# Grouping the rows of two score rings by head, with the block-diagonal pads as plain copies

## The chip, the cores and the metric

The kernel runs on one core of one Trainium2 chip. The time is the device time of one execution in microseconds (us), as a median over several runs. A core has five engines that run their own instruction streams and wait for each other by semaphores: TensorE (PE, matmuls), VectorE (DVE), ScalarE (ACT), GpSimd (POOL) and SyncE (SP, which in this kernel issues nearly all DMAs). Sixteen DMA engines move data between device memory and the on-chip SBUF, which has 128 partitions; matmuls write to PSUM.

## The reference

The input x is one sequence of 2048 rows of 512 numbers. Two branches are mixed by a gate per row:

```python
g = sigmoid((x * gate_w).sum(-1, keepdims=True))
a = einsum("bsd,ed->bse", x, dft_hid_re);  b = einsum("bsd,ed->bse", x, dft_hid_im)
fourier = einsum("ts,bse->bte", dft_seq_re, a) - einsum("ts,bse->bte", dft_seq_im, b)
q, k, v = x @ wqkv                     # 32 heads of 16
scores = q k^T * 16 ** -0.5            # only 0 <= i - j < 256, else -1e9
attention = (softmax(scores) @ v) @ wo
out = g * fourier + (1 - g) * attention
```

So there is a Fourier branch of large dense products, and an attention of 32 small heads with a sliding window of 256 positions.

## The kernel before

**Number form.** Operands of the larger products are kept as a high and a low part in the fp32r type (`hi`, `lo`, `split`), and a product is three matmuls, hi·hi, hi·lo and lo·hi (`TERMS`). This holds for the projections to q, k and v, for the Fourier products and for the output product with wo.

**Attention tiles.** The 32 heads are four groups (`NG`) of four pairs (`NP`) of heads. The sequence is cut in blocks of 64 (`BQ`), so there are 32 blocks (`NB`) per group and 128 in all, counted by n. Two rings in SBUF, `ring[0]` for q and `ring[1]` for k, hold one group's values for 2048 positions; a partition is a row, and the free axis is (pair, position). Each of a pair's two heads has 16 rows of high and 16 of low parts, and rows of high parts are repeated so that one contraction over the partitions sums the three terms. Before the change the rows stand by part: 0-31 the high parts of both heads, 32-63 the low parts or the repeat, 64-95 the rest; rows 96-99 of `ring[0]` hold the row maxima that the transposed scores need.

A *pad* is the small stationary operand of a score matmul: for one block and pair, the columns 0-63 hold the 64 positions with head 0's rows only, and the columns 64-127 the same with head 1's rows only, so that one matmul gives both heads' scores. `make_pad` (L328 to L340) writes it from the ring, for all four pairs at once, by a multiplication with a 0/1 column `half` that blanks the other head's rows: two instructions per pad, of 96 rows each. `pads[0]` (from the q ring) serves `s_pair`, `pads[1]` (from the k ring) serves `t_pair`; there are two buffers of each (`NPAD`), so the pad of block n+2 cannot be written until the matmuls of block n are done. Three of the four instructions per block run on DVE (L339), the second of `pads[1]` on ACT (L337).

**Passes over a block.** `s_pair(n, p)` computes scores of 64 queries against up to 320 keys (L356), adds the mask and takes the minimum on DVE (L358), and exponentiates on ACT with a row sum (L361). Every eight blocks, the maxima and sums are split (`ml_split`), transposed on PE (`ml_turn`), and sent through device memory (`ml_rows`) into the rows of `ring[0]` (`m_ring`, L394). `LAG` = 19 blocks later `t_pair(k, p)` computes the transposed scores, 64 keys by up to 320 queries (L439), with the maxima subtracted in the same contraction, exponentiates on ACT (L440), and POOL zeroes the two triangular corners outside the window (`affine_select`, L445 and L449): two 64-row instructions per corner and two pairs, one for each head, since a head's keys stand in 64 partitions of their own. `pv` (L466) multiplies with v; its stationary operand `vpad` is again block-diagonal, spread by two POOL copies of 64 rows per four blocks (`v_spread`, L423) from `vr`, which two DMAs fill (`v_load`).

**The way of q and k.** A projection of 512 positions is accumulated in PSUM. `qk_evict` (L248) writes the high part with ACT (L84) and the low part with DVE (L86, L88) into one of three rotating slots of the tile `home`, and stores it to device memory (`qk_scr`) with one DMA of 128 partitions (512 KB). `ring_load` (L280) then brings q and k of 512 positions into the rings with four DMAs, of 64, 32, 32 and 64 partitions (512 or 256 KB). There are 16 ring loads, four per group. All these DMAs, and `ld` in general (L56), are issued by SP in program order, so one that waits holds up those behind it.

**Dense work between.** `dense()` is a generator that yields one matmul of the projections and Fourier products at a time. The main loop runs over n, and per pair emits the s matmul of block n, some dense matmuls (`fill`, 3 to 4 per pair), the t matmul of block n - 19, and more dense ones. The order on PE is thereby written out by hand. In the first part (L142 to L159) the orders of ACT, DVE and SP are, too; later they are set by a scheduler on estimated times, and `behind(...)` only fixes that an instruction is issued after the one marked last on an engine. The Fourier products over the sequence (`dc`) take their stationary operands from `raw` tiles with pieces of `cr` and `ci`, loaded and split one piece ahead (`Pieces`).

**Setup.** POOL builds the mask, the identity, `half` and `mrow`, zeroes rows 96-127 of the rings (`clear_rows`, L189), the corresponding rows of `pads`, and `vpad`; `clear_pads` (L201) sets rows of ones in `pads[1]`, to which the maxima rows of `ring[0]` answer.

Of the kernel before, what the change touches and what calls it, by code (L numbers as in the profile page):

```python
# [7 lines left out]
F32 = mybir.dt.float32  # L8
# [24 lines left out]
def fnet_window_mix(ctx: ExitStack, tc: tile.TileContext, xT, x, wqk, wv, wr, wi, cr, ci, wo, gw, out):  # L33
# [12 lines left out]
    qk_scr = [[[dram.tile([2, P, 512], F32, name=f"qk_scr{i}_{g}_{c}") for c in range(4)]  # L46
# [11 lines left out]
    def f(ap):  # L58
        return ap.bitcast(F32)
# [119 lines left out]
    half = const.tile([P, 2], F32, name="half")  # L179
    mrow = const.tile([P, 2], F32, name="mrow")  # L180
    for t, edges in ((half, ((0, 16, 32, 48, 64, 80), (16, 32, 48, 64, 80, 96))), (mrow, ((96, 98), (98, 100)))):
        nc.gpsimd.memset(t, 0.0)
        for h in range(2):
            for i, e in enumerate(edges[h]):
                a = t[:, h:h + 1]
                nc.gpsimd.affine_select(a, a, pattern=[[0, 1]], compare_op=OP.is_ge, fill=1.0 - i % 2,
                                        base=e - 1, channel_multiplier=-1)

    def clear_rows(i, ss):  # L189
        with behind("pool"):  # L190
            nc.gpsimd.memset(f(ring[i][96:128, :, ss * 512:(ss + 1) * 512]), 0.0)

    first_lo = f(XT[0, 0][96:128, 1]).rearrange("r (p c) -> r p c", p=NP)
    for t in pads[0]:
        mark("pool", nc.gpsimd.affine_select(t[96:128], first_lo, pattern=[[0, NP], [0, P]], compare_op=OP.is_gt,
                                             fill=0.0, base=0, channel_multiplier=0))
# [4 lines left out]
    def clear_pads():  # L201
        for t in vpad:
            nc.gpsimd.memset(t, 0.0)
        for t in pads[1]:
            nc.gpsimd.memset(f(t[96:128]), 1.0)
            for h in range(2):
                a = t[96:128, :, 64 * h:64 * h + 64]
                nc.vector.tensor_scalar(a, f(a), mrow[96:128, h:h + 1], None, op0=OP.mult)
# [39 lines left out]
    def qk_evict(g, ss, i, ps):  # L248
        hl = hl_tile()
        split_psum(hl[:, 0], hl[:, 1], ps, -SCALE if i == 0 else 1.0)  # L250
        ld(qk_scr[i][g][ss].rearrange("h x s -> x h s"), f(hl[:]))
# [76 lines left out]
    def make_pad(i, n):  # L328
        if not 0 <= n < NG * NB:
            return  # L330
        t = pads[i][n % NPAD]
        b = n % NB
        with behind(*(("act", "dve") if n < NPAD else ())):
            for h in range(2):
                src, dst = f(ring[i][:96, :, b * BQ:(b + 1) * BQ]), t[:96, :, 64 * h:64 * h + 64]
                if i and h:
                    nc.scalar.activation(dst, src, AF.Copy, scale=half[:96, h:h + 1])  # L337
                else:
                    nc.vector.tensor_scalar(dst, src, half[:96, h:h + 1], None, op0=OP.mult)  # L339
        PAD[i, n] = t  # L340
# [5 lines left out]
    def s_pair(n, p):  # L346
# [9 lines left out]
        nc.tensor.matmul(ps[:, :w], PAD[0, n][:, p], ring[1][:, p, k0:k0 + w], start=True, stop=True)  # L356
# [49 lines left out]
    def v_load(n):  # L406
        if n >= NG * NB:
            return
        g, kb = divmod(n, NB)
        raw = at.tile([P, 4, 64], F32, name="vr", bufs=1)  # L410
        for h in range(2):
            ld(raw[64 * h:64 * h + 64].rearrange("r (c j) x -> r c j x", j=2),
               v_scr[kb // 4][:, :, h, g, :].rearrange("c (j r) x -> r c j x", r=64))
        VR[n] = raw

    def v_spread(n):
# [4 lines left out]
        for h in range(2):  # L421
            r = slice(64 * h, 64 * h + 64)
            nc.gpsimd.tensor_copy(v2[r, :, :, 16 * h:16 * h + 16], raw[r].rearrange("r j (p d) -> r j p d", d=16))  # L423
        V2[n // 4] = v2

    def t_pair(n, p):
# [12 lines left out]
        nc.tensor.matmul(ps[:, :w], PAD[1, n][:, p], ring[0][:, p, q0:q0 + w], start=True, stop=True)  # L439
        nc.scalar.activation(pt[:, p, :w], ps[:, :w], AF.Exp, scale=-1.0)  # L440
        if p % 2:
            ph = slice(p - 1, p + 1)
            for h in (0, 64):
                a = pt[h:h + 64, ph, 0:64]
                nc.gpsimd.affine_select(a, a, pattern=[[0, 2], [1, 64]], compare_op=OP.is_ge, fill=0.0,  # L445
                                        base=0, channel_multiplier=-1)
                if w == WIN:
                    a = pt[h:h + 64, ph, 256:320]
                    nc.gpsimd.affine_select(a, a, pattern=[[0, 2], [-1, 64]], compare_op=OP.is_gt, fill=0.0,  # L449
                                            base=0, channel_multiplier=1)  # L450
# [479 lines left out]
```

## Time and profile before

| | |
|---|---|
| time, median of 3 runs | 853.65 us (852.76 to 855.3) |
| the profiled execution's own time | 853.36 us |
| its span in the profile | 851.3 us |
| PE busy | 844.4 us (99%) |
| DVE busy | 618.0 us (73%) |
| ACT busy | 592.0 us (70%) |
| POOL busy | 373.5 us (44%) |
| granted PE clock | 1.0 |
| moved by DMA | 161.03 MB, mean 189 GB/s |

A line of a group reads: line of the code, engine, operation, output tile <- input tiles, the shape (partitions x elements), the count, then busy time and mean ns of one, and the idle time of the engine just before them with what ended it. A line of a timeline gives the start, the duration and, in square brackets, the idle time before and who ended it. PE, DVE, ACT and POOL stand for the engines, PEld for loading a matmul's stationary operand, SPq for the DMA issues of SP. Matmuls overlap one another in the pipeline, so from one start to the next is less than the duration shown.

### The profile page before, as it was taken

The page shows a single profiled execution, that of the slowest core. Times are in us where ns is not written, and L with a number is a line of the kernel's source. Part 1 is how long each engine was busy: PE and PEld are TensorE (multiplying, and loading weights), DVE is VectorE, ACT ScalarE, POOL GpSimd, SP SyncE. Part 2 cuts the span into 40 slices and gives each one's busy share as a digit, 9 for nine tenths or more (in the row PEclk, how much of TensorE's full clock was granted, in tenths as well). Part 3 has the DMA queues.
Part 4 walks back from the last instruction along what each step waited for, and adds up shares of the span by engine and source line. Part 5 has one row for each costly group of instructions (what it writes and reads, how often), then busy time and mean ns, then how long its engine had stood idle before and what let it go on. Part 6 is the DMA issues. An engine that isn't in the chain of part 4 may idle for free.

```text
span 851.3 us, 17207 instructions
## 1 busy us (share of the span) xinstructions
PE 844.4 (99%) x5166; PEld 691.0 (81%) x5166; DVE 618.0 (73%) x2011; ACT 592.0 (70%) x1793; POOL 373.5 (44%) x1067
## 2 busy tenths in 40 slices
PE   8999999999999999999999999999999999999998
PEld 6888788788778888888878887888888887878887
DVE  5588978767878777769777787788888774447531
ACT  5488898888888987779778887778777765532200
POOL 9100244444543555456535546555355577740000
PEclk9999999999999999999999999999999999999999
DMA  7876577576675265444545556989774345359543
GB/s 247 284 235 203 179 247 237 205 238 215 208 240 173 68 210 122 153 129 139 154 114 151 164 144 205 294 275 287 254 216 145 111 148 162 120 170 317 159 147 98
DMA packets 94861, 161.03 MB, mean 189 GB/s; under 512 B 27312, under 2 KB 36272, under 8 KB 94768
## 3 DMA queue, kind: packets, MB, share of 16 engines
q1 hardware_dynamic: 94336, 159.28, 60.0%
q8 instruction: 40, 0.66, 0.3%
q10 hardware_dynamic: 432, 0.66, 0.2%
q14 instruction: 53, 0.43, 0.2%
HBM read 108.27 MB, written 51.64 MB: 188 GB/s over the span
## 4 chain that ended last, share of the span: by engine, by line
PE 94%; DVE 3%; DMA 2%; issue 1%; ACT 0%; SPq 0%; DVEq 0%; ACTq 0%
PE dc L518 41%; PE dab L294 10%; PE s L356 8%; PE o L466 8%; PE t L439 8%; PE dqk L271 7%; PE dv L294 5%; PE t L788 5%; DMA qk_scr<-home 1%; DVE sm L358 1%; DMA pt<-wqk 1%; PE s L259 0%; DVE pad L339 0%; DVE home L88 0%; DVE hi L574 0%
## 5 line engine op out<-in xcount | busy, mean ns | idle before, releaser
L361 ACT ACTIVATE sm<-sm,ml 128x320 f32<-128x320 f32 (+4 forms) x512 | 278.0, 544 | 101.7 <-DVE ml L358 96.5
L518 PE MATMUL dc<-big,hi 128*128 128x512 f32 x1020 | 344.4, 393 | 0.0
L358 DVE CUSTOM_DVE_ANT_0 sm<-s,mask 128x320 f32<-128x320 f32 (+4 forms) x512 | 235.1, 463 | 110.4 <-PE s L356 87.7
L445 POOL TENSOR_SCALAR_AFFINE_SELECT pt<-pt 64x128 f32<-64x128 f32 x392 | 137.1, 350 | 225.7 <-ACT pt L440 213.6
L518 PE MATMUL dc<-big,lo 128*128 128x512 f32 x510 | 200.6, 393 | 0.0
L518 PEld LDWEIGHTS dc<-big,hi 128*128 128x128 f32 x1020 | 179.7, 188 | 21.4
L440 ACT ACTIVATE pt<-t 128x320 f32<-128x320 f32 (+4 forms) x392 | 160.5, 411 | 43.9 <-PE t L439 41.2
L356 PE MATMUL s<-ring,pad 128*128 128x320 f32 (+4 forms) x512 | 157.6, 308 | 0.0
L439 PE MATMUL t<-ring,pad 128*128 128x320 f32 (+4 forms) x512 | 154.2, 301 | 0.0
L339 DVE TENSOR_SCALAR pad<-ring,half 96x256 fp32r<-96x256 f32 x384 | 119.9, 358 | 13.0 <-PE t L439 12.8
L356 PEld LDWEIGHTS s<-ring,pad 128*128 128x128 f32 x512 | 96.1, 188 | 30.2 <-issue 9.0
L449 POOL TENSOR_SCALAR_AFFINE_SELECT pt<-pt 64x128 f32<-64x128 f32 x344 | 119.7, 348 | 0.1
L439 PEld LDWEIGHTS t<-ring,pad 128*128 128x128 f32 x512 | 96.1, 188 | 21.9 <-DVE ml L358 0.7
L518 PEld LDWEIGHTS dc<-big,lo 128*128 128x128 f32 x510 | 95.8, 188 | 13.8 <-issue 1.6
L574 DVE TENSOR_TENSOR lo<-raw,hi 128x512 fp32r<-128x512 f32 x142 | 97.8, 698 | 0.1
L361 ACT ACTIVATION_READ_ACCUMULATOR sm<-sm,ml 128x1 f32 x512 | 97.6, 191 | 0.0
L294 PE MATMUL dab<-hi,big 128*128 128x512 f32 x256 | 89.4, 394 | 0.1
L271 PE MATMUL dqk<-big,hi 128*128 128x512 f32 x240 | 85.5, 394 | 0.8 <-DVE home L86 0.7
L423 POOL COPY vpad<-vr 64x256 f32<-64x256 f32 x64 | 27.7, 433 | 108.5 <-DMA vr<-v_scr 81.7
L574 DVE CAST hi<-raw 128x512 fp32r<-128x512 f32 x142 | 60.8, 437 | 18.9 <-PE dc L518 11.7
L445 POOL TENSOR_SCALAR_AFFINE_SELECT home<-home 64x128 f32<-64x128 f32 x120 | 44.3, 369 | 55.0 <-ACT home L440 47.9
L337 ACT ACTIVATE pad<-ring,half 96x256 fp32r<-96x256 f32 x128 | 63.9, 499 | 0.0
(96 smaller groups left out, 959.5 us busy)
## 6 DMA issues: line engine op xcount, KB each, us to landing
qk_scr<-home SPq DMA_DIRECT2D x32, 512.0 KB
ring<-qk_scr SPq DMA_DIRECT2D x32, 512.0 KB
raw<-cr SPq DMA_DIRECT2D x32, 512.0 KB
raw<-ci SPq DMA_DIRECT2D x32, 512.0 KB
r_scr<-ev SPq DMA_DIRECT2D x42, 256.0 KB
ev<-r_scr SPq DMA_DIRECT2D x42, 256.0 KB
ab_scr<-home SPq DMA_DIRECT2D x20, 512.0 KB
big<-ab_scr SPq DMA_DIRECT2D x20, 512.0 KB
```

The source lines that it names most:

```text
L271: nc.tensor.matmul(ps, w[a][:, c:c + 128], XT[dk, ss][:, b], start=n == 0, stop=n == 11)
L294: nc.tensor.matmul(ps, XT[dk, ss][:, a, c * 128:(c + 1) * 128], wh[b], start=n == 0, stop=n == 11)
L339: nc.vector.tensor_scalar(dst, src, half[:96, h:h + 1], None, op0=OP.mult)
L356: nc.tensor.matmul(ps[:, :w], PAD[0, n][:, p], ring[1][:, p, k0:k0 + w], start=True, stop=True)
L358: mark("dve", nc.vector.tensor_tensor_reduce(out=sm[:, :w], in0=ps[:, :w], in1=mask[:, WIN - w:], scale=1.0, scalar=3e38, op0=OP.add, op1= ...
L361: mark("act", nc.scalar.activation(sm[:, :w], sm[:, :w], AF.Exp, bias=nm[:, c], scale=-1.0, accum_out=l[:, c]))
L439: nc.tensor.matmul(ps[:, :w], PAD[1, n][:, p], ring[0][:, p, q0:q0 + w], start=True, stop=True)
L440: nc.scalar.activation(pt[:, p, :w], ps[:, :w], AF.Exp, scale=-1.0)
L445: nc.gpsimd.affine_select(a, a, pattern=[[0, 2], [1, 64]], compare_op=OP.is_ge, fill=0.0, base=0, channel_multiplier=-1)
L449: nc.gpsimd.affine_select(a, a, pattern=[[0, 2], [-1, 64]], compare_op=OP.is_gt, fill=0.0, base=0, channel_multiplier=1)
L518: nc.tensor.matmul(ps, w[a][:, i % 8 * 128:i % 8 * 128 + 128], ab[SC[i]][:, b], start=i == ends[0] and a + b == 0, stop=i == ends[1] and a ...
L574: return fn(*args)
```

## The change

The rows of rings and pads are grouped by head: head h has the 48 rows 64h to 64h+47, and the two maxima rows of a head follow at 64h+48. Rows between are zero in the pads. Then a block-diagonal pad is two plain copies of 48 rows, and nothing is to be blanked.

- `make_pad`: `pads[0]` is two DVE copies; `pads[1]` is two GpSimd copies, whose output has a stride of two, since in `pads[1]` the two heads now alternate: column 2r + h is key r of head h. ACT has no part of it any more.
- The transposed scores have keys of the two heads in alternating partitions, so one `affine_select` over 128 partitions per corner zeroes both heads' corners: half as many instructions as before.
- `v_load` is one DMA, and `v_spread` multiplies all 128 rows by the 0/1 column `side`, twice.
- `qk_scr` has an axis for the head; a store is two DMAs of 64 partitions (256 KB each) instead of one of 128. `ring_load` is eight DMAs, of 32, 16, 16 and 32 rows for each head, instead of four. `m_ring` is two DMAs of two rows instead of one of four.
- The s matmul contracts over 112 rows and the t matmul over 114, instead of 128.
- `half` and `mrow` are gone; `side` is a reduction of the identity on DVE and one more small instruction. `clear_rows` zeroes rows 32-63, before the ring loads write some of them; `clear_pads` sets ones and takes the other rows away with selects.

On PE the order of all matmuls is the same in both kernels. On SP two loads of `x` that stood ahead of a qk store near the end of the second group's projections stand behind it. POOL's pad copies stand among the selects of the block before, and the first of a pair waits for the t matmuls that last read its buffer.

```diff
 def clear_rows(i, ss):
-            nc.gpsimd.memset(f(ring[i][96:128, :, ss * 512:(ss + 1) * 512]), 0.0)
+            nc.gpsimd.memset(f(ring[i][32:64, :, ss * 512:(ss + 1) * 512]), 0.0)
...
 def qk_evict(g, ss, i, ps):
-        ld(qk_scr[i][g][ss].rearrange("h x s -> x h s"), f(hl[:]))
+        for h in range(2):
+            ld(qk_scr[i][g][ss][h].rearrange("a x s -> x a s"), f(hl[64 * h:64 * h + 64]))
...
 def ring_load(g, ss):
-        q, k = (qk_scr[i][g][ss].rearrange("h (x p) s -> (h x) p s", p=NP) for i in range(2))
-        ld(f(ring[0][0:64, :, sl]), q)
-        ld(f(ring[1][0:32, :, sl]), k[0:32])
-        ld(f(ring[0][64:96, :, sl]), q[0:32])
-        ld(f(ring[1][32:96, :, sl]), k)
+        for h in range(2):
+            r = 64 * h
+            q, k = (qk_scr[i][g][ss][h].rearrange("a (x p) s -> (a x) p s", p=NP) for i in range(2))
+            ld(f(ring[0][r:r + 32, :, sl]), q)
+            ld(f(ring[1][r:r + 16, :, sl]), k[0:16])
+            ld(f(ring[0][r + 32:r + 48, :, sl]), q[0:16])
+            ld(f(ring[1][r + 16:r + 48, :, sl]), k)
...
 def make_pad(i, n):
-                src, dst = f(ring[i][:96, :, b * BQ:(b + 1) * BQ]), t[:96, :, 64 * h:64 * h + 64]
-                if i and h:
-                    nc.scalar.activation(dst, src, AF.Copy, scale=half[:96, h:h + 1])
+                r = slice(64 * h, 64 * h + 48)
+                src = f(ring[i][r, :, b * BQ:(b + 1) * BQ])
+                if i:
+                    nc.gpsimd.tensor_copy(turned(t)[r, :, :, h], src)
                 else:
-                    nc.vector.tensor_scalar(dst, src, half[:96, h:h + 1], None, op0=OP.mult)
+                    nc.vector.tensor_copy(t[r, :, 64 * h:64 * h + 64], src)
...
 def s_pair(n, p):
-        nc.tensor.matmul(ps[:, :w], PAD[0, n][:, p], ring[1][:, p, k0:k0 + w], start=True, stop=True)
+        nc.tensor.matmul(ps[:, :w], PAD[0, n][:112, p], ring[1][:112, p, k0:k0 + w], start=True, stop=True)
...
 def m_ring(u):
-            ld(f(ring[0][96:100, :, U * 512:(U + 1) * 512]), m_scr[u])
+            for h in range(2):
+                ld(f(ring[0][64 * h + 48:64 * h + 50, :, U * 512:(U + 1) * 512]), m_scr[u][2 * h:2 * h + 2])
...
 def v_spread(n):
         for h in range(2):
-            r = slice(64 * h, 64 * h + 64)
-            nc.gpsimd.tensor_copy(v2[r, :, :, 16 * h:16 * h + 16], raw[r].rearrange("r j (p d) -> r j p d", d=16))
+            nc.gpsimd.tensor_scalar(v2[:, :, :, 16 * h:16 * h + 16], raw.rearrange("r j (p d) -> r j p d", d=16),
+                                    side[:, h:h + 1], None, op0=OP.mult)
...
 def t_pair(n, p):
-        nc.tensor.matmul(ps[:, :w], PAD[1, n][:, p], ring[0][:, p, q0:q0 + w], start=True, stop=True)
+        nc.tensor.matmul(ps[:, :w], PAD[1, n][:114, p], ring[0][:114, p, q0:q0 + w], start=True, stop=True)
-            for h in (0, 64):
-                a = pt[h:h + 64, ph, 0:64]
-                nc.gpsimd.affine_select(a, a, pattern=[[0, 2], [1, 64]], compare_op=OP.is_ge, fill=0.0,
-                                        base=0, channel_multiplier=-1)
+            a = pt[:, ph, 0:64]
+            nc.gpsimd.affine_select(a, a, pattern=[[0, 2], [2, 64]], compare_op=OP.is_ge, fill=0.0,
+                                    base=1, channel_multiplier=-1)
```

The new helper `turned(t)` views a pad's 128 columns as 64 pairs: `t[:].rearrange("x p (r h) -> x p r h", h=2)`.

More of the change, by code (lines that the diff above doesn't have):

```diff
@@ L44, in fnet_window_mix @@
     dram = ctx.enter_context(tc.tile_pool(name="dram", bufs=1, space=DRAM))
-    qk_scr = [[[dram.tile([2, P, 512], F32, name=f"qk_scr{i}_{g}_{c}") for c in range(4)]
+    qk_scr = [[[dram.tile([2, 2, 64, 512], F32, name=f"qk_scr{i}_{g}_{c}") for c in range(4)]
                for g in range(NG)] for i in range(2)]
@@ L410, in v_load @@
         raw = at.tile([P, 4, 64], F32, name="vr", bufs=1)
-        for h in range(2):
-            ld(raw[64 * h:64 * h + 64].rearrange("r (c j) x -> r c j x", j=2),
-               v_scr[kb // 4][:, :, h, g, :].rearrange("c (j r) x -> r c j x", r=64))
+        ld(raw.rearrange("r (c j) x -> r c j x", j=2),
+           v_scr[kb // 4].rearrange("c (j r) h g x -> g (r h) c j x", r=64)[g])
         VR[n] = raw
```

37 lines of the change are left out of this document (17 added, 20 removed).

## The prediction

> **What bounds the kernel.** I read the page first, then busy time by stage, then the waits around the stages where TensorE (PE) is not full.
>
> ```profile
> span 851.3 us, 17207 instructions
> PE 844.4 (99%) x5166; PEld 691.0 (81%) x5166; DVE 618.0 (73%) x2011; ACT 592.0 (70%) x1793; POOL 373.5 (44%) x1067
> PE 94%; DVE 3%; DMA 2%; issue 1%; ACT 0%; SPq 0%; DVEq 0%; ACTq 0%
> ```
>
> ```profile
> 20.00:60.00 40.00, 40.00 (x189) 33.11 (x188) 28.07 (x104) 23.82 (x74) 5.32 (x12) 1.00 0.85 271
> 60.00:100.00 40.00, 38.80 (x188) 32.65 (x187) 36.53 (x141) 33.45 (x102) 0.86 (x3) 1.00 0.57 181
> 100.00:140.00 40.00, 39.94 (x243) 32.20 (x242) 32.27 (x112) 34.75 (x108) 20.13 (x60) 1.00 0.75 244
> 140.00:700.00 560.00, 559.89 (x3650) 459.82 (x3652) 442.89 (x1520) 447.61 (x1397) 284.41 (x836) 1.00 0.59 183
> 700.00:760.00 60.00, 60.00 (x445) 47.76 (x435) 27.23 (x54) 31.10 (x76) 42.20 (x121) 1.00 0.43 138
> ```
>
> The columns are the window, its length, then busy time of PE, weight loads, VectorE (DVE), ScalarE (ACT) and GpSimd (POOL), the granted clock, and DMA share and GB/s. PE is the bound everywhere at clock 1.00. From 20 to 760 us it is idle 1.20 + 0.06 + 0.11 = 1.4 us. The matmuls of the changed kernel are as many and as wide, so whatever relieves another engine can win at most about 1.4 us. What makes a transfer or a copy late has no such cap.
>
> **Relief of DVE and ACT.** Before, a block (64 keys or queries of 8 heads) has three pad copies on DVE and one on ACT; after, it has two shorter ones on DVE (pad 0) and two on POOL (pad 1).
>
> ```profile
> L339 DVE TENSOR_SCALAR pad<-ring,half x384: 332/345/510, 33.8 to 754.1; 96x256 fp32r<-96x256 f32 x192
> ...
> L337 ACT ACTIVATE pad<-ring,half 96x256 fp32r<-96x256 f32 x128 | 63.9, 499 | 0.0
> ...
> L369 DVE CAST mlh<-ml x16: 181/191/320, 63.5 to 690.1; 128x64 fp32r<-128x64 f32 x16
> ...
> L80 DVE CAST big<-raw x8: 417/421/427, 23.6 to 52.2; 128x512 fp32r<-128x512 f32 x8
> ```
>
> ```profile
> 93.55 0.27 PE L376 MATMUL s<-ident,mlh 128*64 128x128 f32 x1 [0.54 <-DVE mlh L370]
> ...
> 99.31 0.50 PE L271 MATMUL dqk<-big,hi 128*128 128x512 f32 x1 [0.65 <-DVE home L86]
> ```
>
> A plain copy of 256 elements is interpolated between the CASTs: 191 + 192 x (421 - 191)/448 = 290 ns against 345. Until pad 1 begins, a block saves DVE 2 x 55 ns = 0.11 us; from then on 3 x 345 - 2 x 290 = 0.455 us. ACT loses its 63.9 us, which free no PE time as ACT is 0% of the chain above. The two PE waits on DVE shown fall at 93.55, where one or two blocks' 0.11 us can have gathered (I take 0.15 of the 0.54), and at 99.31, where pad 1 has begun (one and a half blocks' 0.455, so nearly all of the 0.65: 0.6). Term: **-0.75 us** (bounds 0 and -1.4).
>
> **GpSimd.** It gains two pad copies per block and loses half its selects, each twice as many partitions.
>
> ```profile
> L423 POOL COPY vpad<-vr x64: 390/399/1263, 90.2 to 740.5; 64x256 f32<-64x256 f32 x64
> ...
> L445 POOL TENSOR_SCALAR_AFFINE_SELECT pt<-pt x392: 286/293/1148, 102.8 to 763.8; 64x128 f32<-64x128 f32 x196
> ...
> L176 POOL TENSOR_SCALAR_AFFINE_SELECT ident<-ident x1: 294/294/294, 2.5 to 2.5; 128x128 fp32r<-128x128 f32 x1
> ```
>
> ```profile
> 8.65 14.08 POOL L191 MEMSET ring<- 32x2048 f32 x8
> ...
> 724.53 0.85 POOL L423 COPY vpad<-vr 64x256 f32<-64x256 f32 x2 [1.50 <-DMA vr<-v_scr]
> ```
>
> ```profile
> 7.06 1.15 DVE L81 TENSOR_TENSOR big<-pt,big 128x512 fp32r<-128x512 f32 x1 [1.20 <-ACT big L78]
> ```
>
> A select of 128 partitions costs what one of 64 does (294 against 293 ns); so a block's POOL work goes from 8 x 0.293 = 2.34 us to 4 x 0.294 + 2 x 0.399 = 1.97 us. No row has the strided output of pad 1; at the longest copy, 1.263 us each, a block would be 3.7 us, and the 128 blocks (selects from 102.8 to 763.8) are 5.2 us apart. In the end phase, 700 to 760 us, they are nearer: 121 POOL instructions are some 15 blocks, 4 us each with 42.20/15 = 2.8 us of POOL work, which becomes 2.8 x 1.97/2.34 = 2.4. A pad-1 copy waits for the last t of block k and is needed by the first t of block k + 2, so about a block lies between: hidden. Behind a waiting copy on POOL stand the next selects, for which pv waits some blocks later: hidden too. The thin place is the end, where v_spread waits for its load (the 1.50 above) and pad copies queue behind it; without cover that costs its 1.5 us there. The v_spread instructions stay 64, now of 128 partitions at the price of 64, as the selects show. The zeroing of the ring (14.08/8 = 1.76 us each) must now precede the ring loads; the two that matter end near 8.65 + 3.52 = 12.2 us, and the loads issue at 19.67 (below): hidden by 7 us, also with the pads' longer clearing ahead of it. Term: **0** (0 to +1.5). The new reduce and scalar on DVE fall into its startup idle of 1.20 us (last row): 0; without that cover they would be two small instructions, under 0.4 us by the 191 ns CAST.
>
> **Matmul rows.** s and t contract over 112 and 114 rows instead of 128.
>
> ```profile
> 97.90 0.31 PE L356 MATMUL s<-ring,pad 128*128 128x320 f32 x1
> 98.04 0.39 PE L271 MATMUL dqk<-big,hi 128*128 128x512 f32 x1
> 98.27 0.39 PE L271 MATMUL dqk<-big,lo 128*128 128x512 f32 x1
> ```
>
> All rows of the trace contract over 128, so they do not price this. Start to start, 320 columns take 0.14 us and 512 columns 0.23, the same time per column: the width sets it, and I take **0** (no row suggests a loss; the gain, if rows counted, is a rival). The Trainium skill, "TensorE: Matmul & The Clock Gate", section on LDWEIGHTS, says the row count does not matter for a weight load; no run here shows it yet.
>
> **Transfers.** The ring load (1.573 MB for 512 positions) was four DMAs over partitions 0-63, 0-31, 64-95 and 32-95; it becomes eight, of 32, 16, 16 and 32 rows, each wholly in 0-63 or wholly in 64-127. The qk store (0.524 MB) was one DMA over 128 partitions; it becomes two of 64.
>
> ```profile
> 19.67 3.16 SPq L56 DMA_DIRECT2D ring<-qk_scr  x4
> ...
> 25.38 0.39 SPq L56 DMA_DIRECT2D raw<-xT  x1
> ```
>
> ```profile
> 33.17 0.76 DVE L80 CAST big<-raw 128x512 fp32r<-128x512 f32 x2 [2.96 <-DMA raw<-xT]
> 33.85 0.60 DVE L339 TENSOR_SCALAR pad<-ring,half 96x256 fp32r<-96x256 f32 x2
> ```
>
> ```profile
> 34.51 0.30 PE L356 MATMUL s<-ring,pad 128*128 128x64 f32 x1
> ```
>
> ```profile
> 24.00:25.00 1.00, 1.00 (x6) 0.84 (x5) 0.96 (x3) 0.03 (x1) 1.00 (x4) 1.00 1.06 203
> ...
> 32.00:33.00 1.00, 1.00 (x7) 0.81 (x6) 0.00 (x0) 0.19 (x1) 0.00 (x0) 1.00 1.04 404
> ```
>
> ```profile
> 50.00:51.00 1.00, 1.00 (x6) 0.83 (x5) 1.00 (x4) 0.80 (x3) 0.00 (x0) 1.00 1.03 217
> 51.00:52.00 1.00, 1.00 (x7) 0.87 (x6) 1.00 (x5) 1.00 (x4) 0.00 (x0) 1.00 1.06 221
> 52.00:53.00 1.00, 1.00 (x7) 0.83 (x6) 1.00 (x5) 1.00 (x4) 0.00 (x0) 1.00 1.07 229
> ```
>
> With the DMA engines full (share 1.0 and above), the kernel moves 404 GB/s while xT lands on 128 partitions, and about 222 GB/s (217, 221, 229) while a ring load's one-sided pieces land. By these two rates a ring load before is (0.524 + 0.262 + 0.262)/0.222 + 0.524/0.404 = 6.0 us, the last piece straddling both sides; after it is 1.573/0.222 = 7.1 us: **+1.1**. A qk store goes from 0.524/0.404 = 1.3 to 2.36 us: **+1.06**. Bounds: if consecutive pieces of opposite sides overlap, a ring load is 1.573/0.404 = 3.9 us (-2.1) and a store +0. If 16 rows run at half of 32 rows' rate again, four of the eight pieces (0.524 MB) take another 2.36 us: +3.5. I take one after another at 222, the rate that both a 64-row and a 32-row piece show.
>
> *Start.* Two stores and one ring load stand in the queue before the xT load, whose landing lets DVE cast at 33.17, then copy the pad at 33.85, then PE do its first s at 34.51, back to back: no slack. Extra: 2 x 1.06 + 1.1 = **+3.2 us** (0 to +5.6; a gain is worth nothing, since PE runs full up to there). SP issues six DMAs more at about 3.16/4 = 0.79 us, 4.7 us, which moves the issue of xT (25.38) by at most that; it lands almost 8 us after its issue, behind what is queued, so the transfers and not SP set it. The v stores behind it on SP are read some 50 us later (first v copy at 90.2).
>
> *Group turn near 110 us.* PE resumes at 118.02 on a chain whose longest piece is a transfer:
>
> ```profile
> 103.59 2.77 SPq L56 DMA_DIRECT2D ring<-qk_scr  x4
> 106.46 1.02 SPq L56 DMA_DIRECT2D raw<-x  x2
> ```
>
> ```profile
> 107.58 8.98 DMA qk_scr<-home
> ...
> 116.64 0.61 ACT home L84
> ...
> 117.27 0.70 DVE home L88
> ...
> 118.02 0.49 PE dab L294
> ```
>
> The store issued at 107.58 has the store before it, a ring load and raw<-x ahead of it, and the next eviction needs its slot of home. Extra: 2 x 1.06 + 1.1 = 3.2; the two raw<-x loads (0.524 MB, 1.3 us at 404) are now queued behind, so **+1.9 us** (0 to +4.3).
>
> *Later ring loads.* Of the others, those in the dc phase stand before loads of cr and ci, which the pieces are split from with one piece of lead; the trace has one place where the cast waits:
>
> ```profile
> 592.22 0.43 DVE L574 CAST hi<-raw 128x512 fp32r<-128x512 f32 x1 [0.61 <-DMA raw<-ci]
> ```
>
> The load is late there and PE does not stall, so +1.1 is mostly covered: **+0.2** (0 to +2). The m_ring pieces (+16 DMAs) and the v loads (-32) hang on nothing near.
>
> **Sum** against the profiled execution's 853.36 us (span 851.3; the median of the runs is 853.65, 0.3 above): 853.36 - 0.75 + 0 + 0 + 3.2 + 1.9 + 0.2 = 857.9, rounded to 858.0.
>
> **Rivals.**
> *The 16-row pieces halve again.* Then a ring load costs +3.5, the start 2 x 1.06 + 3.5 = +5.6 and the turn 5.6 - 1.3 = +4.3: 853.36 - 0.75 + 5.6 + 4.3 + 0.2 = 862.7. For it: rows fell from 404 to 222 when partitions halved from 128 to 64. Against: 32-row pieces at 52 us run no slower than 64-row ones (229 against 217). Chance 0.22. The Trainium skill, "SBUF — State Buffer", "Door 1: The DMA port swizzle", makes the rate go by how many of 16 ports the partitions reach: rows 0-31 or 0-63 reach eight, rows 0-15 or 32-47 four; by it the sum would be this rival's. The trace agrees for eight against sixteen; none of its large transfers reach just four.
>
> *The transfers are hidden or the sides overlap.* For it: DMA share 0.57 to 0.85 leaves room, and 16 engines each with a queue of its own need not stay in step. Against: the full share at 24 to 34 us with no slack behind. Only the relief is left: 853.36 - 0.75 + 0.2 = 852.8. Chance 0.27.
>
> *Faster: rows count.* If a matmul's time falls with the rows it contracts, 1024 matmuls at 0.14 us of spacing (143 us together) save up to 12%, 17 us; it decides from 7.1 us on, 5% of them, since 4.5 is needed to undo the sum above and 2.6 more to be seen: 853.36 - 0.75 + 5.3 - 17 = 841 at the most. For it: no row excludes it. Against: the equal time per column above. Chance 0.06.
>
> *GpSimd late at the end or at every block.* With copies of 1.26 us a block of the end phase has 2.4 + 2 x 0.86 = 4.1 us of POOL work in 4 us, and t waits from there on: about 0.1 us a block and 1.5 us at each of three or four v_spreads, on hidden transfers 852.8 + 1.5 + 3 x 1.5 = 858.8. Chance 0.06.
>
> **How the numbers follow.** Main forecast 0.39. The 0.3% that a measurement tells from no change is 2.6 us. Slower: main 0.36 (its low end, with part of the transfers hidden, is within: 0.03), halving 0.22, GpSimd 0.05 = 0.63. Same: 0.03 + 0.25 + 0.01 = 0.29. Faster: rows 0.06 and 0.02 of the hidden case = 0.08. The main case's own range is 855.5 to 860.5. The range 852.0 to 863.5 leaves out the rows case, the lowest of the hidden one and the highest of the halving.
>
> **What would show it.** Right: in the 24 to 34 us windows the rate stays near 220 GB/s for over 7 us; the first s stands about 3 us later; the store at the group turn lands later than 8.98 us after issue and PE waits there; pad copies on DVE near 290 ns and no PE wait on POOL. Wrong: s and t spaced closer, the first s still at 34.5, waits of t on POOL, or rates above 300 GB/s while a ring load lands.

## The result: 28 us slower, and the profile after

The changed kernel takes 882.41 us (median of 4 runs, 880.75 to 894.15), against 854.19 us of the kernel before: a ratio of 1.0316, 95% interval 1.0285 to 1.0346. In a second set of runs it took 881.80 us against 853.10, a ratio of 1.0329 (1.0265 to 1.0393). The direction was forecast; the size, 858.0 us with a range up to 863.5, was not.

One of the first four executions, that of 894.15 us, was in a slower state and the ratio leaves it out; as the first profile is of that execution, the lines below are from the second profile, of an execution of 879.73 us. From the page of the changed kernel, the span, the engines and the chain:

```profile
span 878.0 us, 16821 instructions
...
PE 860.1 (98%) x5166; PEld 697.6 (79%) x5166; DVE 610.4 (70%) x1881; ACT 552.6 (63%) x1665; POOL 355.1 (40%) x831
...
PE 83%; DMA 8%; DVE 3%; issue 2%; SPq 2%; ACT 1%; POOL 1%; DVEq 0%; ACTq 0%
```

Busy time by stage (window, length, PE, weight loads, DVE, ACT, POOL, granted clock, DMA share, GB/s):

```profile
20.00:60.00 40.00, 36.40 (x170) 29.87 (x169) 24.21 (x89) 20.34 (x64) 5.85 (x9) 1.00 0.86 213
60.00:100.00 40.00, 38.59 (x184) 31.95 (x183) 33.87 (x132) 31.47 (x101) 1.86 (x2) 1.00 0.84 212
100.00:140.00 40.00, 36.79 (x185) 28.94 (x184) 29.39 (x95) 29.45 (x90) 12.30 (x32) 0.96 0.84 213
140.00:700.00 560.00, 555.98 (x3553) 452.72 (x3554) 431.41 (x1395) 411.16 (x1277) 260.57 (x634) 1.00 0.67 183
```

Two things are to be seen, against the first profile of the kernel before. The span grew by 26.7 us, but PE's idle time only by about 11 us (878.0 - 860.1 = 17.9 against 6.9): PE's *busy* time grew by 15.7 us, for the same 5166 instructions. And the DMA engines are busier for what they move: in the stage from 20 us the share is the same, 0.86 for 0.85, at 213 GB/s instead of 271; in the next it rose from 0.57 to 0.84 while the rate rose only from 181 to 212. The busy time is made up of longer steps at the s and t matmuls (experiment 5) and of a lower clock after standstills (the last point of the steps below).

The three longest places where PE stands still and the kernel before does not, then what ended them. At the start xT lands behind the ring load; at the group turn a store of q or k does; in the dc phase a piece of cr:

```profile
38.07 0.27 PE L358 MATMUL s<-ring,pad 112*128 112x64 f32 x1 [1.83 <-issue]
...
125.54 0.42 PE L441 MATMUL t<-ring,pad 114*128 114x320 f32 x1 [2.78 <-ACT pt L442]
...
566.65 0.51 PE L441 MATMUL t<-ring,pad 114*128 114x320 f32 x1 [2.80 <-DVE ml L360]
```

```profile
36.69 0.76 DVE L80 CAST big<-raw 128x512 fp32r<-128x512 f32 x2 [4.75 <-DMA raw<-xT]
...
565.13 0.43 DVE L575 CAST hi<-raw 128x512 fp32r<-128x512 f32 x1 [4.11 <-DMA raw<-cr]
```

```profile
109.51 7.00 DMA ring<-qk_scr
116.53 7.40 DMA qk_scr<-home
...
554.23 10.88 DMA raw<-cr
...
565.48 0.28 DVE pad L341
```

In the last chain DVE's cast waits for the piece of cr, and behind the cast, in DVE's order, stand a pad copy and the mask of s, without which the next matmul has no PSUM slot.

Where the time is lost becomes plain when each matmul of PE, whose order is the same in all these kernels, is compared with the same matmul in the second profile of the kernel before (span 852.9, experiment 11). The lag is how much later it starts, in us, worked out from the start times in the traces:

```
matmul no. (its time before)   changed   before, 112/114 rows   changed, 128 rows and transfers of before
  80  ( 23.2 us)                 -0.3           0.0                   0.1
 150  ( 40.3 us)                  1.9           0.2                  -1.8
 500  (114.2 us)                  3.5           0.5                  -1.8
 600  (131.4 us)                  8.4           0.8                  -1.7
3300  (543.4 us)                 14.8           6.9                  -1.8
3500  (571.9 us)                 19.5           7.1                  -1.8
4460  (720.2 us)                 23.5          10.4                  -1.8
```

The changed kernel loses in steps at the start, the group turn and the first ring load of the dc phase, and besides at a steady rate between 131 and 543 us, where no standstill is. The other two columns are the experiments that took these two losses apart (5 and 8). The -1.8 of the last column is mostly the kernel before: its second profile has a standstill of 1.60 us that ends at 27.27 us, and its first profile and the kernel of the last column have none there.

### The profile page after: what moved, and what is told of

It reads as the page before. It is cut to its first block, busy times and chain, and to the rows that moved or that the text cites. A ratio compares the mean times of both kernels' runs of the same rounds, so it can differ in the third digit from the quotient of the medians.

```text
span 892.4 us, 16821 instructions
## 1 busy us (share of the span) xinstructions
PE 864.6 (97%) x5166; PEld 699.5 (78%) x5166; DVE 610.4 (68%) x1881; ACT 552.9 (62%) x1665; POOL 357.1 (40%) x831
## 4 chain that ended last, share of the span: by engine, by line
PE 84%; DMA 10%; DVE 3%; issue 1%; POOL 1%; ACT 1%; SPq 0%; DVEq 0%; ACTq 0%; POOLq 0%
PE dc L519 35%; PE dab L295 9%; PE s L358 8%; PE dqk L270 8%; PE o L467 7%; PE t L441 7%; PE t L789 5%; PE dv L295 4%; DMA raw<-ci 2%; DMA ring<-qk_scr 2%; DMA vr<-v_scr 2%; DMA raw<-cr 1%; DMA raw<-xT 1%; DMA qk_scr<-home 1%; DVE sm L360 1%
## 5 line engine op out<-in xcount | busy, mean ns | idle before, releaser
L441 PE MATMUL t<-ring,pad 114*128 114x320 f32 (+4 forms) x512 | 156.7, 306 | 15.8 <-DVE ml L360 9.7
L339 POOL CAST pad<-ring 48x256 fp32r<-48x256 f32 x256 | 124.6, 487 | 107.3 <-PE t L441 87.8
L358 PE MATMUL s<-ring,pad 112*128 112x320 f32 (+4 forms) x512 | 159.5, 311 | 4.3 <-DVE pad L341 3.6
L446 POOL TENSOR_SCALAR_AFFINE_SELECT pt<-pt 128x128 f32<-128x128 f32 x196 | 65.1, 332 | 166.7 <-ACT pt L442 160.8
L441 PEld LDWEIGHTS t<-ring,pad 114*128 114x128 f32 x512 | 96.4, 188 | 39.8 <-DVE ml L360 10.6
L358 PEld LDWEIGHTS s<-ring,pad 112*128 112x128 f32 x512 | 96.6, 189 | 36.3 <-issue 14.2
L424 POOL TENSOR_SCALAR vpad<-vr,side 128x256 f32<-128x256 f32 x64 | 60.6, 957 | 125.6 <-DVE lo L575 63.1
L341 DVE CAST pad<-ring 48x256 fp32r<-48x256 f32 x256 | 98.8, 386 | 6.8 <-DMA ring<-qk_scr 2.9
L442 ACT ACTIVATE home<-t 128x320 f32<-128x320 f32 (+4 forms) x120 | 48.8, 408 | 18.8 <-PE t L441 18.0
L467 PE MATMUL o<-pt,vpad 128*32 128x320 f32 (+4 forms) x1072 | 58.7, 358 | 0.0
```

The lines of the kernel that those rows point to most:

```text
L339: nc.gpsimd.tensor_copy(turned(t)[r, :, :, h], src)
L341: nc.vector.tensor_copy(t[r, :, 64 * h:64 * h + 64], src)
L358: nc.tensor.matmul(ps[:, :w], PAD[0, n][:112, p], ring[1][:112, p, k0:k0 + w], start=True, stop=True)
L441: nc.tensor.matmul(ps[:, :w], PAD[1, n][:114, p], ring[0][:114, p, q0:q0 + w], start=True, stop=True)
L467: nc.tensor.matmul(OT[g, sb][32 * p:32 * p + 32, q - sb * 512:e - sb * 512], v2[:, p], pt[:, p, q - q0:e - q0], start=first, stop=kb == 8 ...
```

## The experiments

Theories: A, the shapes of the transfers make loads late; B, GpSimd's new work makes t late; and, formed later from the traces, C, matmuls over fewer than 128 rows take longer.

**1. The transfers of the change inside the kernel before.** The store as two DMAs of 64 partitions, the ring load as eight pieces, four of them of 16 rows:

```diff
...
-        ld(f(ring[0][0:64, :, sl]), q)
-        ld(f(ring[1][0:32, :, sl]), k[0:32])
-        ld(f(ring[0][64:96, :, sl]), q[0:32])
-        ld(f(ring[1][32:96, :, sl]), k)
+        ld(f(ring[0][0:32, :, sl]), q[0:32])
+        ld(f(ring[1][0:16, :, sl]), k[0:16])
+        ld(f(ring[0][32:48, :, sl]), q[32:48])
+        ld(f(ring[1][32:64, :, sl]), k[0:32])
+        ld(f(ring[0][64:96, :, sl]), q[0:32])
+        ld(f(ring[1][16:32, :, sl]), k[16:32])
+        ld(f(ring[0][48:64, :, sl]), q[48:64])
+        ld(f(ring[1][64:96, :, sl]), k[32:64])
```

> The kernel before, with only its transfers cut like those of the change: the qk store as two DMAs of 64 partitions, the ring load as eight DMAs of 32 and 16 rows, each on one side of partition 64. Layout, pads, selects and matmul rows are those of before. Theory A (the shapes of the transfers cost the time, the 16-row pieces most, through late loads at the start, at the group turn and in the dc phase): 870 to 884 us, with windows near 115 GB/s at a full DMA share while a ring load lands. Theory B (GpSimd's pad copies and its longer v spread make the t matmuls late, the transfers cost only what was forecast for them): 855 to 859 us.

Measured: 866.86 us, ratio 1.0151 (1.0103 to 1.0198), so some 13 us: about half of the loss, and B's 855 to 859 for this kernel is out. Theory A alone, which expected 870 or more, falls short as well.

**2. The same with six pieces of 32 rows** (0-31, 32-63 and 64-95 of each ring).

> The kernel before, with the qk store as two DMAs of 64 partitions and the ring load as six one-sided DMAs of 32 rows, so without 16-row pieces. Theory A, if it is the 16 rows that cost: 855 to 861 us, as the main forecast had it for one-sided pieces at 222 GB/s. If instead one-sided pieces and their number cost as such: 868 us and more. Theory B: 855 to 859 us here as well, and no difference between this and the kernel with 16-row pieces.

Measured: 856.41 us, 1.0031 (1.0008 to 1.0055): 2.6 us. One-sided pieces alone cost little; with 16-row pieces among them it is 10 us more. The rate tells why. One ring load in a quiet stretch, in the second profile of before, then with 32-row pieces, then in the changed kernel:

```profile
52.00:53.00 1.00, 1.00 (x6) 0.83 (x6) 1.00 (x6) 0.79 (x4) 0.00 (x0) 1.00 1.09 231
...
56.00:57.00 1.00, 1.00 (x7) 0.87 (x6) 1.00 (x5) 1.00 (x3) 0.00 (x0) 1.00 1.14 422
```

```profile
57.00:58.00 1.00, 1.00 (x7) 0.82 (x6) 1.00 (x4) 1.00 (x5) 0.00 (x0) 1.00 1.03 193
...
59.00:60.00 1.00, 1.00 (x7) 0.83 (x5) 0.64 (x4) 0.86 (x4) 0.00 (x0) 1.00 1.04 201
```

```profile
55.00:56.00 1.00, 1.00 (x7) 0.83 (x6) 0.96 (x5) 1.00 (x5) 0.00 (x0) 1.00 1.10 111
56.00:57.00 1.00, 1.00 (x6) 0.84 (x5) 1.00 (x6) 0.84 (x5) 0.00 (x0) 1.00 1.05 115
...
60.00:61.00 1.00, 1.00 (x6) 0.83 (x5) 0.66 (x3) 1.00 (x4) 0.00 (x0) 1.00 1.09 111
```

At full DMA share the last column reads some 190 to 230 GB/s for 32 or 64 rows of one side of partition 64, 422 when the piece straddles the two sides, and 111 to 115 for 16 rows. From the landing of the store ahead of it to its last landing the whole ring load takes 5.9 us before, 7.7 us in six pieces of 32, 8.9 us with the eight pieces of experiment 1, and 11.2 us in the changed kernel, whose eight pieces have the same sizes but stand four on one side of partition 64 and then four on the other. This is the rule of the Trainium skill, "SBUF — State Buffer", "Door 1: The DMA port swizzle" (four ports for 16 rows, eight for 32 or 64, sixteen for both sides), and the runs agree with it.

**3. Pieces of 48 rows, first attempt.** The scratch holds a third row group per head, and a store is three DMAs of 128 partitions whose target has the head as its outer dimension.

> The changed kernel, with its layout, pads, selects and matmul rows, but the qk scratch holds three row groups per head, so that the ring load is four DMAs of 48 rows and the qk store three DMAs over 128 partitions (half as many bytes again in the store). Theory A: the 16-row pieces are gone, ring loads take about 7 us each, time 854 to 860 us. Theory B: what GpSimd does is unchanged, so 875 us and more.

Measured: 1249.83 us, 1.4623 (1.4574 to 1.4672). It says nothing on the theories, since the new form of the store was slow itself: its DMAs ran at 53 GB/s with a DMA share of 0.14, about two engines of sixteen, and SP and PE stood.

```profile
32.00:33.00 1.00, 0.00 (x0) 0.00 (x0) 0.00 (x0) 0.00 (x0) 0.00 (x0) 0.50 0.14 53
```

An outer dimension of two got two engines. The Trainium skill, "DMA: Bandwidth & Descriptors", says under "How many engines (k)" that the number must divide the slowest dimension of both sides; the row agrees.

**4. The changed kernel again**, for the profile used above.

> The changed kernel itself, on the chip of the three others and beside the same runs of before. Both theories: 881 us, 1.032 of before. It is run for a profile in which the places where TensorE stands still can be compared with those of the other three.

**5. Only the contraction rows, in the kernel before.** Its steps from a 128-row matmul to one over 112 or 114 rows, and back, looked longer in the changed kernel's traces: medians of 231 and 232 ns for 226, and 151 and 152 for 146, from start times.

```diff
-        nc.tensor.matmul(ps[:, :w], PAD[0, n][:, p], ring[1][:, p, k0:k0 + w], start=True, stop=True)
+        nc.tensor.matmul(ps[:, :w], PAD[0, n][:112, p], ring[1][:112, p, k0:k0 + w], start=True, stop=True)
...
-        nc.tensor.matmul(ps[:, :w], PAD[1, n][:, p], ring[0][:, p, q0:q0 + w], start=True, stop=True)
+        nc.tensor.matmul(ps[:, :w], PAD[1, n][:114, p], ring[0][:114, p, q0:q0 + w], start=True, stop=True)
```

> The kernel before, with only the contraction rows of the changed kernel: s matmuls over 112 rows and t matmuls over 114 instead of 128 (the rows left out are zero in it). Theory C (in the traces of the changed kernel, each step from a matmul over 128 rows to one over 112 or 114, and back, is some 5 to 6 ns longer than the same step before, 226 to 232 and 146 to 151 ns; with 1024 s and t matmuls that is some 10 us): 862 to 866 us, all of it as longer steps, no new standstill. Theory A (all by the transfers and the clock): 853 us.

Measured: 863.96 us, 1.0127 (1.0108 to 1.0146): 9.9 us for an edit that takes work away. The page shows it as busy time; the kernel before in its second profile, then this one:

```profile
span 852.9 us, 17207 instructions
...
PE 845.2 (99%) x5166; PEld 692.1 (81%) x5166; DVE 617.5 (72%) x2011; ACT 591.6 (69%) x1793; POOL 371.2 (44%) x1067
```

```profile
span 864.1 us, 17207 instructions
...
PE 855.9 (99%) x5166; PEld 695.9 (81%) x5166; DVE 618.5 (72%) x2011; ACT 594.8 (69%) x1793; POOL 367.1 (42%) x1067
```

PE's busy time is 10.7 us longer, its idle time 0.5; the clock is 1.0 in both. Two steps for each of 1024 matmuls at 5 to 6 ns are 10 to 12 us. Theory C holds.

**6. What number of rows does it?** s over 127 rows and t over 100, in the kernel before.

> The kernel before with s matmuls over 127 rows and t matmuls over 100. It is to tell what the longer steps go by. If any number under 128 costs the same 5 to 6 ns per step: s and t steps both 231 and 151 ns, about 863 us. If the cost grows with the rows left out: none to speak of for s, and 10 ns or more for t.

Measured: 867.21 us in one run, and the same steps: 231 and 151 ns at the s matmuls of 127 rows, 232 and 152 at the t matmuls of 100. So for s one row less costs what 16 less cost, and for t 28 less cost what 14 did. The time is some 4 us over the 863 expected; this profile has a standstill of 3.08 us that ends at 28.78 us, where experiment 5 has one of 1.78. Whether the weight load or the matmul itself makes the step longer, and whether it would also be longer in a stream in which all matmuls had fewer than 128 rows, no run shows.

**7. The changed kernel with 128 rows.** In a first form, the rows that came in were zeroed by eight more memsets.

> The changed kernel, with s and t matmuls over all 128 rows; the rows that this takes in are zeroed at the start on GpSimd (eight memsets more). Theory C: 10 us less than the changed kernel, 869 to 873 us. Theory A alone: 881 us.

> The same with 128 rows, and with the transfers of the kernel before: one store of 128 partitions and four ring loads of 64, 32, 32 and 64 partitions. It leaves the grouping by head out of the rings, so their rows do not match the pads and the attention's numbers mean nothing; every engine's instructions but the transfers are those of the changed kernel. Theory A and C together: 851 to 855 us. Theory B (GpSimd's pad copies and longer v spread cost time of their own): 858 us and more, with waits of t matmuls for pads on GpSimd.

> The changed kernel with 128 rows, and the eight pieces of a ring load issued in turns of the two sides (q rows of head 0, then of head 1, and so on, the k pieces of 32 rows before the 16-row ones), same pieces and bytes. If pieces of opposite sides that follow each other overlap in the DMA engines: 858 to 864 us, with 200 GB/s and more while a ring load lands. If they run one after another whatever their order: as with 128 rows alone, 869 to 873 us.

Measured: 877.31 us (1.0288, 1.0247 to 1.0329), 859.75 (1.0077, 1.0060 to 1.0095) and 866.80 (1.0168, 1.0113 to 1.0223). Each is some 3 to 5 us above the range of the theory that was to hold, and the second lies in the range of B. All three carry a cost of the experiment at the start, shown here for the second: sixteen memsets of the ring kept POOL busy up to 39.5 us, and two casts on DVE, 0.76 us together in the changed kernel, and the two pad copies behind them took several times as long.

```profile
9.11 30.35 POOL L190 MEMSET ring<- 32x2048 f32 x16
```

```profile
32.86 2.96 DVE L80 CAST big<-raw 128x512 fp32r<-128x512 f32 x2 [0.64 <-DMA raw<-xT]
35.74 3.86 DVE L339 CAST pad<-ring 48x256 fp32r<-48x256 f32 x2
```

Eight memsets over all 128 partitions do the same without it:

```diff
...
-            nc.gpsimd.memset(f(ring[i][32:64, :, ss * 512:(ss + 1) * 512]), 0.0)
+            nc.gpsimd.memset(f(ring[i][:, :, ss * 512:(ss + 1) * 512]), 0.0)
```

> The changed kernel with s and t matmuls over 128 rows, now with the ring zeroed by eight memsets over all 128 partitions, as many as in the changed kernel. The earlier form had sixteen, which ran on GpSimd up to 39.5 us and while which DVE's casts took 1.4 to 2.1 us instead of 0.42. If that was a cost of the experiment: 871 to 874 us, 4 less than the earlier form and 8 to 10 less than the changed kernel. If the matmul rows are worth only half of it inside the changed kernel: 877 us again.

Measured: 874.77 us, 1.0230 (1.0188 to 1.0272), some 7 us less than the changed kernel's 881.80 in another set of runs. The steady loss is gone: the lag is 14.4 us at the 600th matmul and 14.6 at the 3300th, where the changed kernel went from 8.4 to 14.8. That 7 us is less than 9.9 is in part because, where PE waits for a transfer, a faster PE only waits longer. The first wait of the dc phase here, 2.80 us in the changed kernel:

```profile
568.38 0.63 PE L441 MATMUL t<-ring,pad 128*128 128x320 f32 x1 [4.80 <-DVE ml L360]
```

The start differs as well, most of it before the first s matmul has run: with the same transfers the 150th matmul is 7.2 us late in this profile and 1.9 in the one above. Why, no run shows.

**8. 128 rows and the transfers of before.** As in the second form of experiment 7, the rings are not grouped by head in it, so its attention means nothing, and its times are those of the changed kernel's instructions.

```diff
...
-        for h in range(2):
-            ld(qk_scr[i][g][ss][h].rearrange("a x s -> x a s"), f(hl[64 * h:64 * h + 64]))
+        ld(qk_scr[i][g][ss].rearrange("h x s -> x h s"), f(hl[:]))
...
+        ld(f(ring[0][0:64, :, sl]), q)
+        ld(f(ring[1][0:32, :, sl]), k[0:32])
+        ld(f(ring[0][64:96, :, sl]), q[0:32])
+        ld(f(ring[1][32:96, :, sl]), k)
```

> The same, with the transfers of the kernel before (one store, four ring loads of 64, 32, 32 and 64 partitions); the rings' rows do not match the pads, so the attention's numbers mean nothing, and every engine but the DMAs works as in the changed kernel. If transfers and matmul rows are the whole loss: 852 to 855 us, the same as before. If GpSimd's copies and the longer v spread cost time of their own: 857 us and more, with t matmuls waiting for GpSimd.

Measured: 854.84 us, 1.0007 (0.9988 to 1.0027): what the kernel before takes. Its page, and its line of the pad copies on POOL:

```profile
span 851.6 us, 16671 instructions
```

```profile
L336 POOL CAST pad<-ring x256: 399/417/954, 31.0 to 754.2; 48x256 fp32r<-48x256 f32 x128
```

No matmul waits for these copies in that trace. So without the new transfers and the missing rows nothing is lost, within some 2 us: everything else in the change, GpSimd's copies, half the selects, the longer v spread, less work on DVE and ACT, adds up to nothing by itself. Taken off in this order, the rows are worth 7 us and the transfers 20; in the kernel before, the same kinds of edit cost 9.9 and 13. Theory B falls as a cause of its own. But with the new transfers the pad copies on POOL do cost something: when a load of v lands late, the pad copy behind it on POOL is late too, and t waits for it, in the changed kernel twice:

```profile
658.38 0.41 PE L441 MATMUL t<-ring,pad 114*128 114x320 f32 x1 [1.03 <-POOL pad L339]
...
754.73 0.41 PE L441 MATMUL t<-ring,pad 114*128 114x320 f32 x1 [0.92 <-POOL pad L339]
```

Experiment 1 has the same kinds of transfers without pads on POOL, and no such wait. This and the longer ring load (11.2 us against 8.9) are likely reasons why the transfers cost more in the changed kernel than in the kernel before; how much each is worth was not measured apart.

**9. The pieces in turns of the two sides**, with 128 rows and eight memsets:

```diff
...
+        for i, a, n, src in ((0, 0, 32, 0), (1, 16, 32, 0), (0, 32, 16, 0), (1, 0, 16, 0)):
+            for h in range(2):
+                ld(f(ring[i][64 * h + a:64 * h + a + n, :, sl]), qk[h][i][src:src + n])
```

> The same 128 rows and eight memsets, with the changed kernel's pieces of the ring load issued in turns of the two sides. By the earlier form of it (866.8 us) and what the extra memsets cost: 861 to 864 us.

Measured: 863.96 us, 1.0113 (1.0068 to 1.0158), 11 us less than with head 0's pieces first. The same eight pieces, 7.9 us instead of 11.2 for a ring load in the quiet stretch. There the last pieces, of 16 rows (with the end of a 32-row one in the first line), run at

```profile
60.00:61.00 1.00, 1.00 (x6) 0.82 (x5) 0.94 (x5) 0.75 (x4) 0.00 (x0) 1.00 1.11 188
61.00:62.00 1.00, 1.00 (x7) 0.82 (x6) 0.78 (x4) 1.00 (x3) 0.00 (x0) 1.00 1.00 211
```

near twice the 111 of 16 rows, so short neighbours on opposite sides do overlap; the 32-row ones ahead, at 209 to 234, are hardly faster than on one side. It is the best form of the change that was found, and slower than the kernel before.

**10. Pieces of 48 rows, second attempt**, with one-sided stores (two of 256 KB and two of 128 KB); head 0 first, and in turns.

> The changed kernel with 128 matmul rows and eight memsets, whose qk scratch holds a third row group per head, so that a ring load is four one-sided pieces of 48 rows, head 0's before head 1's; the qk store stays one-sided, as two DMAs of 64 partitions and 256 KB and two of 128 KB. If the 16-row pieces are what the changed transfers cost: 857 to 863 us (all pieces at 222 GB/s; the store has half as many bytes again). If it is the long run of pieces on one side and then on the other: 870 us and more, as with the 16-row pieces.

> The same with the 48-row pieces in turns: q of head 0, q of head 1, k of head 0, k of head 1. If neighbours on opposite sides overlap: 2 to 4 us less than with head 0 first. If not: the same within 2 us.

Measured: 873.27 us (1.0218, 1.0176 to 1.0259) and 870.83 (1.0191, 1.0153 to 1.0229). The expectation of 857 to 863 failed: a 48-row piece is no better than its parts. In turns it is 2.4 us less, at the low edge of what overlap was expected to give, with intervals that overlap: nothing follows from it.

```profile
60.00:61.00 1.00, 1.00 (x6) 0.82 (x6) 1.00 (x6) 0.91 (x4) 0.00 (x0) 1.00 0.99 178
61.00:62.00 1.00, 1.00 (x7) 0.82 (x6) 1.00 (x6) 0.93 (x3) 0.00 (x0) 1.00 1.07 162
```

In these rows it runs at some 170 GB/s, not 222; a 32-row and a 16-row piece one after the other, at 222 and 111, would be 167. By the formula of the Trainium skill, "SBUF — State Buffer", "Door 1: The DMA port swizzle", rows 32 to 47 reach the same four ports as rows 0 to 15, so 32 of the 48 rows share four ports; the rate agrees with that, though no run tested it apart. How much of these times is the store's, with half as many bytes again, stays open.

**11. The kernel before, a second profile.**

> The kernel before once more, for a second profile of it: 853 us. It is to show whether the standstill of about 2 us near 25 us, which most profiles of the experiments have and the first profile of the kernel before has not, belongs to the kernel before as well; then it does not count among what the change costs.

Measured: 854.98 us, and the standstill is there: 1.60 us, ended at 27.27. It comes and goes in the kernel before, is 1.77 us in the changed kernel's second profile, and is not counted.

## Why the prediction was wrong, step by step

- **What bounds the kernel.** Right: PE is the bound, relief has no room, and late transfers have no such cap. The sentence that the matmuls are "as many and as wide" was taken to mean as long, and that was not so.
- **Relief of DVE, -0.75.** Not seen. The copies take 399 ns in the median, not the interpolated 290, and so longer than the 345 of what they replace; why, no run shows. The two waits that were to shrink, 0.54 and 0.65 us, are 0.90 and 0.47 in the kernel with 128 rows and the transfers of before, which is level with the kernel before. A small error.

```profile
L341 DVE CAST pad<-ring x256: 269/399/545, 37.4 to 704.3; 48x256 fp32r<-48x256 f32 x128
```

- **GpSimd, 0.** Right as a sum. The pad copies took 417 ns, as priced; the v spread 925 ns instead of 399, since the price of a select does not hold for a multiplication by a column; it was hidden, with the transfers of before. With those of the change the thin place that the prediction named, a v_spread that waits for its load with pad copies behind it, opened: 1.03 and 0.92 us (experiment 8).
- **Matmul rows, 0.** The first step that failed: 9.9 us in the kernel before. The prediction gave a gain as the only other possibility and set no upper bound, on the ground that no row suggested a loss; but no row had fewer than 128 rows at all, and a price of 5 ns for each of 2048 steps is 10 us. The sentence of the Trainium skill, "TensorE: Matmul & The Clock Gate", section on LDWEIGHTS, that rows do not matter for a weight load, does not speak of what follows it; the runs show the loss.
- **Transfers, +1.1 a ring load and +1.06 a store.** The second step that failed: all pieces were taken at 222 GB/s. That one-sided pieces are slower was right, but the rival that 16 rows halve the rate again is what happened (111 to 115 GB/s). A ring load takes 11.2 us, against 7.1 in the forecast and 9.5 by that rival; which side the neighbouring pieces are on matters too (8.9 in experiment 1, 7.9 in turns).
- **Start, +3.2.** Near in size, in part by luck: 3.5 us by the lag at the 150th matmul against the first profile of before, on which the forecast was made, and 1.9 against the second. With the same transfers it varied widely, up to 7.2 against the second profile in experiment 7's kernel with eight memsets.
- **Group turn, +1.9.** It was 4.9 us (8.4 - 3.5 in the table): 2.78 of standing still, some 1.7 by the clock after it (last point), and the rows.
- **Later ring loads, +0.2 with an upper bound of 2.** The third step that failed: the first ring load of the dc phase costs 4.7 us by itself (19.5 - 14.8), of which 2.80 is standing still and some 1.7 the clock after it. The row at 592.22 showed DVE already waiting for its piece, and how much later than that a load may land before PE waits was not worked out; "mostly covered" had no number under it.
- **Left out: the clock after a standstill.** After PE stood 2.80 us at 566.65 the granted clock fell to half; over the rows below it lost 0.60 + 1.00 + 0.12, some 1.7 us, which are part of the 4.7 above:

```profile
564.00:566.00 2.00, 0.00 (x0) 0.00 (x0) 0.85 (x3) 0.00 (x0) 0.00 (x0) 1.00 1.02 377
566.00:568.00 2.00, 1.35 (x4) 0.98 (x5) 1.97 (x6) 0.98 (x3) 0.32 (x2) 0.70 1.01 332
568.00:570.00 2.00, 2.00 (x7) 1.68 (x6) 1.99 (x9) 1.76 (x7) 0.67 (x3) 0.50 1.07 353
570.00:572.00 2.00, 2.00 (x11) 1.67 (x10) 1.45 (x5) 1.52 (x6) 1.23 (x3) 0.94 0.74 238
```

The third column from the end is the clock: 1.00, 0.70, 0.50, 0.94. The same follows the wait of 2.78 us at 125.54. After the 1.83 us at 38.07 the clock stayed at 1.00. The length alone does not decide it: with 32-row pieces a wait of 1.92 us that ended at 553.95 was followed by a clock of 0.50, and in experiments 6 and 7 waits of 3.08 and 2.40 us that ended at 28.78 and 27.77 were not. The kernel before has no standstill as long in mid-span, so its trace could not show this.

Had the rival of the halved rate been combined with the loss by rows, 862.7 + 10 = 873 us. Most of the rest to 881 is, by the trace, the dc phase (4.7 us in place of 0.2, the clock included) and the two waits for pads on POOL (2.0).

## What to carry to other kernels

A DMA's rate goes by which partitions it touches, not only by its bytes: regrouping rows for the compute engines can halve or quarter it, and the loss appears far away, in whatever load is queued behind. Filling a contraction up to all 128 rows with zeros was cheaper here than leaving rows out, because each step between matmuls of 128 and of fewer rows cost 5 to 6 ns. Where PE is full, price a late load twice: the standstill, and the clock after it, which fell after some of these waits and not after others.

## What was not expected of the hardware

- A matmul over fewer than 128 rows between matmuls over 128 makes both steps 5 to 6 ns longer (226 to 231 or 232 ns, 146 to 151 or 152), at 127 rows (s) as at 100 (t).
- Short pieces on opposite sides of partition 64, issued in turns, overlap: 188 to 211 GB/s, against 111 for 16 rows one after another on one side. The Trainium skill, "SBUF — State Buffer", "Can I just issue two DMAs to hit both halves?", has only 6% for two such DMAs; for 16-row pieces these rows differ, and for the 32-row ones (209 to 234 GB/s) they agree.
- While POOL ran its sixteen memsets of the ring, DVE's casts of 128x512 took up to 2.11 us (two together 2.96) instead of 0.42; one in the same stretch took 0.49.
- A store with an outer dimension of two moved 53 GB/s at a DMA share of 0.14.
